# Retention and a gated-GELU MLP in fp32 on one core: three quarters of block 1's first product by seven products instead of eight, and a new order of the first steps

## The chip, the cores and the metric

The kernel runs on one core of a Trainium2 chip. The metric is the device time of one execution in microseconds. The engines are called TensorE (PE, with its weight loads PEld), VectorE (DVE), ScalarE (ACT), GpSimd (POOL) and SyncE (SP), which here only issues transfers.

## The reference

Four sequences of 768 positions go through eight heads of a recurrent retention of width 64. Its output, 3072 tokens of 512 numbers, goes through two matrices with a gate h * sigmoid(1.702 h) between them. All is float32.

```python
state = gamma * state + outer(k_t, v_t)          # per batch and head
y_t   = (1/8) * q_t @ state
x     = y, rearranged to (4*768, 8*64) = (3072, 512)
h     = x @ w_in                                 # (3072, 2048)
g     = h * (1 / (1 + exp(-1.702 * h)))
out   = g @ w_out                                # (3072, 512)
```

The weights come in as 64-bit floats and are narrowed to 32 bits on the chip.

## The kernel before

Tokens are worked on in six blocks of 512 (`CB` = 4 chunks of 128). A chunk is one of 12 pieces of 64 positions of two sequences; its attention is called a step. Block m+1's attention stands between the matmuls of block m's second product. Blocks 0 and 1 are different from the rest: while their attention and first products run, the weights are still being loaded and narrowed.

Matrices are split in two by two quarters. A product of two such matrices needs eight products of quarters, or seven if sums of quarters are formed first (the Winograd form of Strassen's scheme). The code keeps seven slots for each matrix: quarters 0 to 3, and sums 4, 5, 6; slot 2 is overwritten by a fourth sum, once nobody wants the quarter.

* `up0` makes a chunk of block 0's first product by plain products, `up1(f)` a chunk of 128 of the 2048 features for block 1: four matmuls of 128x512 (L427) into a PSUM tile `ph`, of tag `x` for even f and `y` for odd. `gate1.f` is ScalarE's gate on it, which writes `G`.
* `up(d)`, for blocks 2 to 5, makes four features' chunks at once by the seven products: 28 matmuls of 128x256 (L472). Three copies by ScalarE (`p1`, `u`, `vv`) and three adds by VectorE combine them. The sums of the weights (`sums_w1`) and of X (`sums_x`) stand in place by then.
* `down(m)` is the second product of blocks 0 and 1 by seven products (L709), each over 8 pairs of rows of W2; `sums_w2`, `sums_w2_t3` and `sums_g` make its sums on VectorE. A part of `sums_g` and `sums_w1` goes to GpSimd.
* A weight comes by `fetch` (SP, 512 KB in two transfers) to one of three raw places (`RAWS`: W2[:, 4], W2[:, 5], G[:, 6:8]), is begun by ScalarE (`abs`, L207), and finished by VectorE in `half` (L211 to L213) and `rest` (L217, L218, L222). Weights 0 to 7 are W1, 8 to 15 are W2.
* `X1`, block 1's input, lies in W2[:, 6], and is filled by steps 4 to 7 (`output`, called x4 to x7).

PSUM tiles of tags `x` and `y` have two buffers each; the tiles `q_sq` and `k_sq` (two buffers), `kn`, `tmp`, `kT` (one), `o`, `qT`, `at` (two) belong to the attention and to the outputs.

The order of everything up to block 1's gates is a list of words written out by hand. TensorE's order is the program's. `pin` puts an instruction of another engine behind the one that was traced before it on its engine; instructions without it (among them `aged` and `decay` on GpSimd from step 6 on, and the loads of step 8 and later) are placed by the scheduler, and what is pinned behind them goes with them. [...]

```python
for n, unit in enumerate(down(m) if m < 2 else down49(m, *ring)):
    unit()
    if m == 0 and n < NP and n % 2:
        sums_w2(n - 1)
```

Of the kernel before, what the change touches and what calls it, by code (L numbers as in the profile page):

```python
# [9 lines left out]
F32 = mybir.dt.float32  # L10
U32 = mybir.dt.uint32
AF = mybir.ActivationFunctionType
ALU = mybir.AluOpType
P = 128
# [14 lines left out]
def kernel(  # L29
# [29 lines left out]
    pe, act, dve, pool, sp = nc.tensor, nc.scalar, nc.vector, nc.gpsimd, nc.sync  # L59
# [10 lines left out]
    TH = BT // 2  # L70
    NB = NCH // CB
    NFF = DFF // P
    NP = NFF // 2
# [5 lines left out]
    one = ctx.enter_context(tc.tile_pool(name="one", bufs=1))  # L79
    two = ctx.enter_context(tc.tile_pool(name="two", bufs=2))  # L80
# [3 lines left out]
    ps = ctx.enter_context(tc.tile_pool(name="ps", bufs=2, space=bass.MemoryType.PSUM))  # L84
# [13 lines left out]
    G = const.tile([P, NP, 4, TH], F32, name="G")  # L98
    G0 = one.tile([P, 2, TH], F32, name="g0", tag="kd")
    X1 = W2[:, 6].rearrange("p (s c) t -> p s c t", s=4)  # L100
    rowd = const.tile([P, HP, D], F32, name="rowd")
# [3 lines left out]
    whole = const.tile([P, HP], F32, name="whole")  # L105
# [6 lines left out]
    def w1(p):  # L112

        return (W1A, p) if p < NP // 2 else (W1B[p // 2 - 2], p % 2)
# [3 lines left out]
    def pin(i):  # L118
        return tc.keep_in_program_order(i) if ordered[0] else i
# [58 lines left out]
    def fetch(i):  # L178
        x = raw(i).rearrange("p (n two) -> p n two", two=2)
        pin(sp.dma_start(x.rearrange("p (c f) two -> p c f two", c=2) if i < NFF else x, SRC[i]))  # L180
# [96 lines left out]
    def by_half(t, j):  # L277

        return t.rearrange("p s (w t) -> p w s t" if j < NEW else "p (w s) t -> p w s t", w=2)

    def attend(j, f=None):

        pa = ps_a.tile([P, 2, 2, HP, D], F32, name="pa", tag="pa")
        if j is not None:
            PA[j] = pa
            kt, qt = by_half(KT.pop(j), j), by_half(QT[j], j)
            for s in range(HP):
                for u, w in TWO:
                    pe.matmul(pa[HALF[w], u, 0, s, :], kt[HALF[u], w, s, :], qt[HALF[u], w, s, :], start=True, stop=True)  # L289
        if f is not None:  # L290
            c = f % NC
            old, vn, a, qt = state[c % 2], QKV.pop(("v", f)), AT.pop(f), by_half(QT.pop(f), f)
            if c < NC - 1:
                kd = KD.pop(f)
                for s in range(HP):
                    for w, u in TWO:
                        pe.matmul(pa[HALF[u], w, 1, s, :], kd[HALF[w], HP * u + s, :], vn[HALF[w], HP * u + s, :],
                                  start=True, stop=True)


            py = ps_a.tile([P, 2, 2, 4, D], F32, name="py", tag="py")
            if c:
                for s2 in range(2):
                    for w in range(2):
                        for u, o in TWO:
                            pe.matmul(py[HALF[o], u, 1, 2 * w + s2, :], old[HALF[u], w, 2 * s2 + o, :],  # L306
                                      qt[HALF[u], w, 2 * s2 + o, :], start=True, stop=True)
            for s2 in range(2):
                for u in range(2):
                    for w, o in TWO:  # L310
                        s = 2 * s2 + o
                        pe.matmul(py[HALF[o], w, 0, 2 * u + s2 if f < NEW else 2 * s2 + u, :],  # L312
                                  vn[HALF[w], HP * u + s, :], a[HALF[w], u, s, :], start=True, stop=True)
            PU[f], PY[f] = pa[:, :, 1], py
# [75 lines left out]
    def hidden(g, h):  # L390

        for g, i in g if isinstance(g, list) else [(g, slice(0, 2))]:
            pin(act.activation(g, h[:, i], AF.Gelu_apprx_sigmoid))  # L393
# [34 lines left out]
        return G[:, p, ab:4:2, :], h  # L428


    def sums_w1(p):
        t, q1 = w1(p)
        w = [t[:, q1:q1 + 2, s] for s in range(7)]
        pool.tensor_add(w[4], w[2], w[3])
        pool.tensor_sub(w[6], w[0], w[2])
        pool.tensor_sub(w[5], w[4], w[0])
        pool.tensor_sub(w[2], w[1], w[5])
# [310 lines left out]
    works, products = {}, {}  # L748
# [63 lines left out]
    for j in range(2 * CB):  # L812
        for name in "qkv":
            works[f"{name}{j}"] = lambda j=j, name=name: load(j, name)
        works |= {f"{name}{j}": lambda j=j, do=do: do(j) for name, do in (
            ("turn", turn), ("turned", turned), ("decay", decay), ("masked", masked), ("state", by_state),
            ("x", output), ("aged", aged), ("updated", updated))}
        for f in (None, *range(2 * CB)):
            works[f"step{j}" + ("" if f is None else f"-{f}")] = lambda j=j, f=f: attend(j, f)
        works[f"step-{j}"] = lambda j=j: attend(None, j)  # L820
    for i in range(2 * NFF):
        works[f"w{i // 2}{'ab'[i % 2]}"] = lambda i=i: fetch(i)
    for name, i in [("0a", 0), ("0b", 1)] + [(str(p), 2 * p) for p in range(1, NFF)]:
        n = Narrow(i)
# [19 lines left out]
    begin()  # L844
    for name in """
        k0 table q0 warm turn0 w0b rows warm k1 abs0b q1 turned0 step0 v0 w0a half0b mask k2 turn1 causal rest0b
        masked0 decay0 v1 decay1 abs0a half0a step-0 updated0 turned1 q2 step1 rowd whole w2b turn2 w2a x0 k3
        aged1 masked1 turned2 v2 rest0a abs2 q3 step-1 updated1 state1 decay2 aged2 step2 q4 x1 half2 decay3 w3b
        w3a up0.0.0 masked2 turn3 k4 step-2 v3 q5 rest2 k5 gate0.0.0 turned3 updated2 state2 step3 up0.0.2
        masked3 abs3 half3 x2 rest3 turn4 w1b step-3 aged3 gate0.0.2 turned4 state3 w1a w5b updated3 v5 decay4  # L850
        abs1 x3 turn5 half1 up0.0.3 turned5 up0.1.2 step4 aged4 w5a rest1 v4 gate0.0.3 decay5 w6a masked4
        gate0.1.2 abs5 w6b step5-4 half5 rest5 up0.0.1 updated4 abs6 state4 gate0.0.1 w4b
        up0.1.1 half6 aged5 w4a up0.0.5 rest6 masked5 up0.1.5 gate0.1.1 x4 gate0.0.5 abs4 step-5 w8b w8a
        half4 gate0.1.5 state5 updated5 anew q6 up0.1.6 x5 rest4 gate0.1.6 abs8 v6 up0.0.6 w7b w7a half8
        turn6 gate0.0.6 up0.1.0 abs7 half7 gate0.1.0 w9b w9a up0.1.4 q7 gate0.1.4 decay6 step6 masked6 rest7 up0.0.4 v7
        gate0.0.4 turn7 up0.1.3 gate0.1.3 aged6 step7-6 masked7 updated6 decay7 abs9 state6 x6 up0.0.7 rest8 gate0.0.7
        w11a w11b step-7 state7 x7 half9 w10b w10a up0.1.7 rest9 gate0.1.7 abs11 half11 up1.8 gate1.8
        w12a w12b rest11 up1.5 gate1.5 up1.4 gate1.4 abs10 half10 up1.0 gate1.0 rest10 up1.3 gate1.3 abs12
        aged7 updated7 up1.2 gate1.2 w14b w14a half12 up1.6 gate1.6 rest12 up1.9 gate1.9 abs14 half14 w13a w13b
        up1.11 gate1.11 rest14 up1.10 gate1.10 abs13 half13 w15a w15b up1.7 gate1.7 rest13 abs15 half15 up1.12  # L860
        gate1.12 late_loads up1.13 gate1.13 rest15 up1.15 gate1.15 up1.14 gate1.14 up1.1 gate1.1
    """.split():
        works[name]()
    ordered[0] = False
    INNER = [(0, 19), (0, 22), (0, 26), (1, 2), (1, 12), (1, 15), (1, 18)]
    for m in range(NB):
# [30 lines left out]
# [4 lines that stand above are left out]
            if m == 0 and NP <= n < 3 * NP // 2:  # L901
                sums_w2_t3(2 * (n - NP))
            if m == 1 and n % 8 == 3:
                sums_w1(n // 4)
            if (m, n) in INNER:
                inner_w2(INNER.index((m, n)))
            if between and (n in (2, 5, 11, 16, 21) if m == 1 else n % 3 == (1 if m else 2)):
                between.pop(0)()
            if 0 < m < NB - 1 and n == (23 if m == 1 else 11):
                sums_x()  # L910
# [46 lines left out]
```

## Time and profile before

| what | value |
|---|---|
| median of three runs | 667.8 us (666.75 to 668.11) |
| the profiled execution | 667.55 us, span 665.8 us |
| granted clock of TensorE | 0.995 of full |
| block 1's first product (L427) | 104.17 to 159.11 us |
| the second product of block 0 (L709) begins | 159.11 us |
| first product of block 2 (L472) begins | 265.94 us |
| L211, L212, L217 on 128x1024 | 0.69 us each |
| L213, L218, L222 on 128x1024 | 1.23 us each |

A line of the timeline has the start and the length in us, the engine, the line of the kernel, the operation, what it writes and reads with the size, and how many it merges; in brackets stand the idle time before it and what ended it. A line of the chain of waits has start, length and what was waited for.

### The profile page before, as it was taken

Reading aid. Unit: us, or ns where it says so; the run is one execution under the profiler, and the core shown is the slowest. Engines: PE = TensorE matmul, PEld = TensorE weight load, DVE = VectorE, ACT = ScalarE, POOL = GpSimd, SP = SyncE. Lnnn points to the kernel's source line nnn. Section 1 sums busy time; section 2 is a strip of 40 time slices with the busy share of each in tenths; the row PEclk is TensorE's granted clock in tenths of the full one; section 3 lists DMA queues with packets and bytes.
Section 4 is the critical chain, followed back from the end, with each engine's and each line's share of the span. In section 5 each row is a group of like instructions: output and inputs, shape, how many; then the busy total and the mean of one; then the engine's idle time right before and its main releaser. Section 6 shows DMA issues by size and latency. Waiting matters only on the chain.

```text
span 665.8 us, 14995 instructions
## 1 busy us (share of the span) xinstructions
PE 645.9 (97%) x6294; PEld 559.1 (84%) x6294; DVE 435.1 (65%) x618; ACT 148.2 (22%) x285; POOL 188.7 (28%) x216
## 2 busy tenths in 40 slices
PE   6789999999999999999999999999999999999997
PEld 3678875446888888888999888999888999988997
DVE  3699878788545775456985354995264995254965
ACT  4674322231000000233100233110233110233110
POOL 6400310000268326100445600354700255500000
PEclk9799999999999999999999999999999999999999
DMA  9996637542203546263385742286652143502142
GB/s 174 205 256 178 186 68 231 166 87 38 43 11 133 172 109 189 56 226 123 89 215 132 230 116 94 75 204 150 189 163 95 62 148 113 222 32 94 49 158 96
DMA packets 146083, 89.48 MB, mean 134 GB/s; under 512 B 131456, under 2 KB 132736, under 8 KB 144992
## 3 DMA queue, kind: packets, MB, share of 16 engines
q1 hardware_dynamic: 135856, 45.19, 30.0%
q0 software_dynamic: 7824, 42.10, 17.8%
q10 hardware_dynamic: 2336, 1.25, 0.6%
q8 instruction: 49, 0.80, 0.5%
q14 instruction: 18, 0.15, 0.1%
HBM read 72.89 MB, written 15.47 MB: 133 GB/s over the span
## 4 chain that ended last, share of the span: by engine, by line
PE 80%; DMA 8%; DVE 4%; SPq 3%; POOL 3%; issue 1%; ACT 0%; DVEq 0%; POOLq 0%; ACTq 0%
PE pq L576 21%; PE px L472 16%; PE pd L709 13%; PE py L472 12%; PE ph L427 8%; PE ph L414 4%; DMA W<-in_moe_w_in_dram 2%; PE pa L289 2%; DMA W<-in_moe_w_out_dram 1%; SPq L157 1%; DMA G<-in_moe_w_in_dram 1%; DMA kn_in<-in_k_dram 1%; PE py L312 1%; PE py L306 1%; DMA k_sq<-in_k_dram 1%
## 5 line engine op out<-in xcount | busy, mean ns | idle before, releaser
L576 PE MATMUL pq<-W,G 128*128 128x128 f32 x672 | 80.5, 276 | 0.7 <-issue 0.7
L545 POOL DMA_DIRECT2D ring<-W2D x28 | 15.4, 552 | 228.9 <-PE px L472 118.2
L576 PEld LDWEIGHTS pq<-W,G 128*128 128x128 f32 x672 | 77.6, 192 | 1.5 <-issue 0.9
L472 PE MATMUL px<-X,W1A 128*128 128x256 f32 x256 | 60.0, 380 | 0.8 <-POOL X L442 0.7
L472 PE MATMUL px<-X,W1B 128*128 128x256 f32 x256 | 59.8, 379 | 0.0
L576 PE MATMUL pq<-ring,own 128*128 128x128 f32 x448 | 59.8, 276 | 0.0
L472 PEld LDWEIGHTS px<-X,W1A 128*128 128x128 f32 x256 | 48.3, 190 | 7.9 <-POOL X L442 1.6
L576 PEld LDWEIGHTS pq<-ring,own 128*128 128x128 f32 x448 | 54.5, 192 | 0.4
L472 PEld LDWEIGHTS px<-X,W1B 128*128 128x128 f32 x256 | 48.6, 190 | 6.7
L709 PE MATMUL pd<-W,G 128*128 128x256 f32 x224 | 49.6, 381 | 0.0
L709 PEld LDWEIGHTS pd<-W,G 128*128 128x128 f32 x224 | 42.2, 190 | 5.8
L472 PE MATMUL py<-X,W1A 128*128 128x256 f32 x192 | 45.4, 379 | 0.0
L472 PE MATMUL py<-X,W1B 128*128 128x256 f32 x192 | 45.4, 379 | 0.0
L393 ACT ACTIVATE G<-G 128x512 f32<-128x512 f32 x48 | 30.2, 630 | 52.0 <-DVE G L482 33.4
L472 PEld LDWEIGHTS py<-X,W1A 128*128 128x128 f32 x192 | 36.5, 190 | 5.0
L472 PEld LDWEIGHTS py<-X,W1B 128*128 128x128 f32 x192 | 36.5, 190 | 4.9
L490 DVE TENSOR_TENSOR t<-py,u 128x512 f32<-128x512 f32 x16 | 11.1, 692 | 33.2 <-PE py L472 33.2
L479 ACT ACTIVATE p<-px 128x512 f32<-128x512 f32 x16 | 9.6, 597 | 94.5 <-PE px L472 94.5
L414 PE MATMUL ph<-X,W1A 128*128 128x256 f32 x128 | 29.0, 382 | 1.4 <-DVE X L347 0.8
L576 PE MATMUL pq<-ring,G 128*128 128x128 f32 x224 | 29.6, 275 | 0.0
L576 PE MATMUL pq<-W,own 128*128 128x128 f32 x224 | 29.6, 275 | 0.0
L504 DVE TENSOR_TENSOR G<-G 128x512 f32<-128x512 f32 (+2 forms) x24 | 12.3, 513 | 25.7 <-ACT G L393 25.7
(207 smaller groups left out, 1168.3 us busy)
## 6 DMA issues: line engine op xcount, KB each, us to landing
ring<-W2D POOLq DMA_DIRECT2D x28, 768.0 KB, 4.7
W1B<-W1D POOLq DMA_DIRECT2D x6, 1792.0 KB, 9.3
W<-in_moe_w_in_dram SPq DMA_DIRECT2D x12, 512.0 KB, 5.3
W<-in_moe_w_out_dram SPq DMA_DIRECT2D x10, 512.0 KB, 5.0
out_dram<-o POOLq DMA_DIRECT2D x20, 256.0 KB, 3.2
q_sq<-in_q_dram SPq DMA_DIRECT2D x144, 32.0 KB, 2.2
k_sq<-in_k_dram SPq DMA_DIRECT2D x144, 32.0 KB, 2.2
v_in<-in_v_dram SPq DMA_DIRECT2D x72, 64.0 KB, 2.7
```

The lines of the kernel that those rows point to most:

```text
L157: tc.keep_in_program_order(sp.dma_start(t[r0:r0 + C4, :, n], src[b + r0 // D, :, t0:t0 + C4, r0 % D:r0 % D + C4] .rearrange("h p d -> p h ...
L289: pe.matmul(pa[HALF[w], u, 0, s, :], kt[HALF[u], w, s, :], qt[HALF[u], w, s, :], start=True, stop=True)
L393: pin(act.activation(g, h[:, i], AF.Gelu_apprx_sigmoid))
L414: pe.matmul(h[:, ab], w, X[:, 2 * th + c // 2, c % 2, :], start=(ab == 0 and c == 0), stop=(c == 3), skip_group_check=True)
L427: pe.matmul(h, w, X1[:, c // 2:4:2, c % 2, :], start=(c == 0), stop=(c == 3))
L472: pe.matmul(acc[:, u, :], t[:, q1 + u, sa, c, :], X[:, sb, c, :], start=(start and u == 0 and c == 0), stop=(stop and c == 1), skip_group_ ...
L479: act.activation(p1, x, AF.Copy)
L490: dve.tensor_add(tt, z, u)
L504: dve.tensor_sub(q[0][1], q[0][0], q[0][1])
L545: pool.dma_start(c, W2D[i])
L576: pe.matmul(p0[:, j, :], a[:, d], w[:, d], start=(new and j == 0 and d == 0), stop=(d == NP // 2 - 1), skip_group_check=True)
L709: pe.matmul(p0[:, n, :], g1(m, p, sa)[:, n * P:(n + 1) * P], W2[:, sb, p, :], start=(new and p == 0 and n == 0), stop=(last and p == NP - ...
```

## The change

Twelve of block 1's sixteen chunks (f = 0 to 11) are made by seven products, in groups of four, in the order d = 2, 0, 1. Chunks 12 to 15 stay as they were. Since W1's rows and X1 are needed as they are, the sums go to tiles that are idle at that time: those of X1 to `q_sq`, `k_sq`, `kn` and `tmp`, those of the weights to `qT`, `at`, `o` and `kT`. All are made by GpSimd: 4 for X1, and 4 for each d. The weights 11, 10, 12, 14, 13, 15 are narrowed between the products, as before, in this order. `late_loads` (step 8's and 9's first loads) moves behind the last of the three groups; decay 3 moves behind the first gate; step-0, turn 1 and step 1 move ahead, and q2 ahead of v1.

```diff
+    def seven_x():
+        for n, (tag, bufs) in ((4, ("q_sq", 2)), (5, ("k_sq", 2)), (6, ("kn", 1)), (2, ("tmp", 1))):
+            SUM_X[n] = two.tile([P, 2, TH], F32, name=f"x{n}", tag=tag, bufs=bufs)
+        for to, a, b in ((SUM_X[4], X1[:, 2], X1[:, 0]), (SUM_X[5], X1[:, 3], SUM_X[4]),
+                         (SUM_X[6], X1[:, 3], X1[:, 2]), (SUM_X[2], X1[:, 1], SUM_X[5])):
+            pin(pool.tensor_sub(to, a, b))
+    def seven_w(d):
+        t, q1 = w1(2 * d)
+        w = [t[:, q1:q1 + 2, s].rearrange("p u c f -> p u (c f)") for s in range(4)]
+        SUM_W[d] = {4: one.tile([P, 2, 2 * P], F32, name="w4", tag="qT", bufs=2),
+                    5: one.tile([P, 2, 2 * P], F32, name="w5", tag="at", bufs=2),
+                    6: two.tile([P, 2, 2 * P], F32, name="w6", tag="o"),
+                    2: one.tile([P, 2, 2 * P], F32, name="w2", tag="kT")}
+        m = SUM_W[d]
+        pin(pool.tensor_add(m[4], w[2], w[3]))
+        pin(pool.tensor_sub(m[5], m[4], w[0]))
+        pin(pool.tensor_sub(m[6], w[0], w[2]))
+        pin(pool.tensor_sub(m[2], w[1], m[5]))
+    def seven(d, k):
+        t, q1 = w1(2 * d)
+        a = [G[:, 2 * d:2 * d + 2, s, :] for s in range(4)]
+        def product(acc, sa, sb, start, stop):
+            for u in range(2):
+                for c in range(2):
+                    w = SUM_W[d][sa][:, u, c * P:(c + 1) * P] if sa in (4, 5, 6, 2) else t[:, q1 + u, sa, c, :]
+                    x = SUM_X[sb][:, c, :] if sb in SUM_X else X1[:, sb, c, :]
+                    pe.matmul(acc[:, u, :], w, x, start=(start and u == 0 and c == 0), stop=(stop and c == 1),
+                              skip_group_check=True)
+        def kept(name, tag, src):
+            SEVEN[name] = one.tile([P, 2, TH], F32, name=name, tag=tag)
+            pin(act.activation(SEVEN[name], src, AF.Copy))
+        if k in (0, 1, 3, 5):
+            SEVEN["x" if k == 0 else f"y{k}"] = ps.tile([P, 2, TH], F32, name="ph", tag="x" if k == 0 else "y")
+        acc = SEVEN[f"y{k}" if k in (1, 3, 5) else "x"]
+        product(acc, (0, 1, 5, 4, 6, 2, 3)[k], (0, 1, 5, 4, 6, 3, 2)[k], k in (0, 1, 3, 5), k in (1, 3, 5, 6))
+        if k == 0:
+            kept("p1", "s1", acc)
+        elif k == 1:
+            pin(dve.tensor_add(a[0], acc, SEVEN["p1"]))
+            hidden(a[0], a[0])
+        elif k == 2:
+            kept("u", "s2", acc)
+        elif k == 3:
+            SEVEN["t"] = one.tile([P, 2, TH], F32, name="t", tag="s1")
+            pin(dve.tensor_add(SEVEN["t"], acc, SEVEN["u"]))
+        elif k == 4:
+            kept("vv", "s3", acc)
+        elif k == 5:
+            pin(dve.tensor_add(a[3], SEVEN["y3"], SEVEN["vv"]))
+            hidden(a[3], a[3])
+            pin(dve.tensor_add(a[2], acc, SEVEN["t"]))
+            hidden(a[2], a[2])
+        else:
+            hidden(a[1], acc)
...
-        masked0 decay0 v1 decay1 abs0a half0a step-0 updated0 turned1 q2 step1 rowd whole w2b turn2 w2a x0 k3
-        aged1 masked1 turned2 v2 rest0a abs2 q3 step-1 updated1 state1 decay2 aged2 step2 q4 x1 half2 decay3 w3b
-        w3a up0.0.0 masked2 turn3 k4 step-2 v3 q5 rest2 k5 gate0.0.0 turned3 updated2 state2 step3 up0.0.2
+        masked0 decay0 q2 v1 step-0 updated0 turned1 decay1 step1 rowd masked1 abs0a half0a whole w2b turn2 w2a x0 k3
+        aged1 turned2 v2 rest0a abs2 q3 step-1 updated1 state1 decay2 aged2 step2 q4 x1 half2 w3b
+        w3a up0.0.0 masked2 turn3 k4 step-2 v3 q5 rest2 k5 turned3 gate0.0.0 decay3 updated2 state2 step3 up0.0.2
...
-        w11a w11b step-7 state7 x7 half9 w10b w10a up0.1.7 rest9 gate0.1.7 abs11 half11 up1.8 gate1.8
-        w12a w12b rest11 up1.5 gate1.5 up1.4 gate1.4 abs10 half10 up1.0 gate1.0 rest10 up1.3 gate1.3 abs12
-        aged7 updated7 up1.2 gate1.2 w14b w14a half12 up1.6 gate1.6 rest12 up1.9 gate1.9 abs14 half14 w13a w13b
-        up1.11 gate1.11 rest14 up1.10 gate1.10 abs13 half13 w15a w15b up1.7 gate1.7 rest13 abs15 half15 up1.12
-        gate1.12 late_loads up1.13 gate1.13 rest15 up1.15 gate1.15 up1.14 gate1.14 up1.1 gate1.1
+        w11a w11b step-7 state7 x7 half9 w10b w10a seven_w2 up0.1.7 rest9 gate0.1.7 abs11
+        seven_x seven2.0 seven2.1 half11 seven2.2 seven2.3 w12a w12b rest11 seven2.4 seven2.5 aged7 seven_w0 abs10 seven2.6
+        seven0.0 seven0.1 half10 seven0.2 seven0.3 rest10 w14b w14a seven0.4 seven0.5 seven_w1 abs12 seven0.6
+        updated7 seven1.0 seven1.1 half12 seven1.2 seven1.3 rest12 w13a w13b seven1.4 abs14 seven1.5 half14
+        seven1.6 up1.12 rest14 gate1.12 abs13 half13 w15a w15b late_loads up1.13 gate1.13 rest13 abs15 half15
+        up1.15 gate1.15 rest15 up1.14 gate1.14
```

In `seven`, `seven2.0` is the first of the seven products of d = 2, and so on. Lines of the changed kernel below `up1` stand 67 later, so that L458 becomes L525.

More of the change, by code (lines that the diff above doesn't have):

```diff
@@ L428, in up1 @@
         return G[:, p, ab:4:2, :], h
+    SUM_X, SUM_W = {}, {}
+    def seven_x():
[16 more added lines that the diff above has]
+        pin(pool.tensor_sub(m[2], w[1], m[5]))
@@ new lines @@
+    SEVEN = {}
+    def seven(d, k):
[34 more added lines that the diff above has]
+            hidden(a[1], acc)
@@ L820 @@
         works[f"step-{j}"] = lambda j=j: attend(None, j)
+    works["seven_x"] = seven_x
+    for d in range(NP // 2):
+        works[f"seven_w{d}"] = lambda d=d: seven_w(d)
+        for n in range(7):
+            works[f"seven{d}.{n}"] = lambda d=d, n=n: seven(d, n)
     for i in range(2 * NFF):
```

## The prediction

> **What bounds the kernel now.** I read the page's busy times first, then TensorE's timeline from 100 us on, then the chain of waits.
>
> ```profile
> PE 645.9 (97%) x6294; PEld 559.1 (84%) x6294; DVE 435.1 (65%) x618; ACT 148.2 (22%) x285; POOL 188.7 (28%) x216
> ```
>
> TensorE is the bound as a whole. In the stage that changes it has no gap, so here a matmul less is time less, as long as nothing else is late:
>
> ```profile
> 104.17 3.60 PE L427 MATMUL ph<-W,W1B 128*128 128x512 f32 x8
> ...
> 155.67 3.60 PE L427 MATMUL ph<-W,W1A 128*128 128x512 f32 x8
> 159.11 3.62 PE L709 MATMUL pd<-W,W1A 128*128 128x256 f32 x16
> ...
> 186.62 1.99 PE L709 MATMUL pd<-W,W1B 128*128 128x256 f32 x8 [0.28 <-DVE W1B L458]
> ...
> 265.94 1.89 PE L472 MATMUL px<-X,W1A 128*128 128x256 f32 x8
> 267.67 1.89 PE L472 MATMUL py<-X,W1A 128*128 128x256 f32 x8
> ```
>
> Each f32 matmul leaves two records. A chunk of L427 (4 matmuls, 8 records) takes 3.433 us from start to start: (159.11-104.17)/16. One of the seven products of a later block (8 records of half the width) takes 267.67-265.94 = 1.73 us; 28 of them, 265.94 to 314.29, give 1.727. In 186.62, VectorE (the sums of G) is already the last to arrive.
>
> In the first 44 us the chain of waits runs through loads of W1:
>
> ```profile
> 8.39 10.16 DMA W<-in_moe_w_in_dram
> ...
> 18.56 8.73 DMA G<-in_moe_w_in_dram
> ...
> 30.56 5.77 DMA W<-in_moe_w_in_dram
> ```
>
> Last, what GpSimd and VectorE do to each other, from their timelines:
>
> ```profile
> 76.58 0.78 DVE L212 TENSOR_SCALAR W<-W 128x1024 uint32<-128x1024 uint32 x1
> 77.39 1.94 DVE L213 SCALAR_TENSOR_TENSOR G<-G,W 128x1024 uint32<-128x1024 uint32 x1
> ...
> 95.21 0.68 DVE L368 TENSOR_TENSOR state<-state,pa 128x512 f32<-128x512 f32 x1
> ```
>
> ```profile
> 76.89 1.35 POOL L274 TENSOR_TENSOR G<-kn_in,cold 128x512 f32<-128x512 f32 x1
> 78.21 2.01 POOL L359 TENSOR_TENSOR state<-state,whole_h 128x512 f32<-128x512 f32 x1
> 95.33 1.04 POOL L274 TENSOR_TENSOR G<-kn_in,cold 128x512 f32<-128x512 f32 x1 [15.11 <-DMA kn_in<-in_k_dram]
> ...
> 190.10 2.48 POOL L434 TENSOR_TENSOR W1B<-W1B 128x512 f32<-128x512 f32 x2
> ```
>
> The bracket has the idle time before an instruction and what ended it. At 77 us L213 needs 1.94 us where it takes 1.23 elsewhere: it starts behind GpSimd's L274, and GpSimd's L359 behind it needs 2.01 instead of 1.04. At 95 us the same L274 beside L368 (which reads PSUM) costs neither anything. A sum such as the new ones takes GpSimd 1.24 us alone (L434).
>
> [...]
>
> **The change part by part.**
>
> *Products.* Removed: 12 chunks, 12 x 3.433 = 41.2 us. Added: 21 products, 21 x 1.727 = 36.3 us. Saved on TensorE: **4.9 us**, if it never waits.
>
> *Sums on GpSimd.* 16 instructions (4 of X1, 4 for each of 3 pairs of chunk rows), 16 x 1.25 = 20 us. In the order in which the changed kernel's instructions stand on POOL, they come after decay 7 (ends 96.4 us): four of seven_w2, aged 7, three of seven_w0, and only then the four of seven_x. TensorE's third product (seven2.2) needs x5, the tenth of these. Alone: 96.4 + 9 x 1.25 + 1.04 = 108.7, and TensorE wants it at 104.17 + 2 x 1.73 = 107.6: 1.1 us late[...]. But VectorE stands in L217 to L222 of rest8 and in half9 and rest9, nine instructions[...]. Both queues are full, so they alternate: a VectorE instruction waits about 0.93 us (1.25 less the 0.3 by which neighbours overlap: L213 above, and pairs of L522 with L436 at 212 us repeat every 1.70 us), a GpSimd one 0.4 to 0.95 us. Ahead of x5, by who stands in front: 0.4, 0.9 and 0.9 for the last three of seven_w2, nothing for aged 7 (VectorE then reads PSUM), 0.4, 0.4 and 0.9 for seven_w0, 0.4 and 0.9 for x4 and x5: 5.2 us, so x5 at 114.0. **TensorE waits 6.4 us.**
>
> *VectorE behind it.* Its nine instructions lose 8 us: rest9 ends at 115.1 instead of 108.0. Then a0 add (0.7), half11 (2.7, waits 1.2), t add (0.7), rest11 (3.2, waits 2.0 behind seven_w0's last and seven_w1), so that the add of a3 ends at 126.2. seven0.1 needs the PSUM tile which that add frees; TensorE comes to it at 114.0 + 6 x 1.73 = 124.4 and **waits 1.8**. The add of a2 ends at 126.9; behind it ScalarE has two gates, abs10 (1.1), gate a1 and the copy p1 of the next pair, 3 us: 129.8. seven0.2 overwrites that PSUM tile, comes to it at 128.0 and **waits 1.85**. From there GpSimd has two sums and aged 8 left and TensorE runs free. Sum: 10.1 waited, 4.9 saved: **5.1 us later** at the end of the twelve chunks.
>
> *The tail on VectorE.* In the old order VectorE had room before the second product (idle 6.6 us until 170.32, 2.4 and 1.0 us after it). Now rest12 to rest15 come late. From the end of seven1.5: two adds 1.8, weight 14 5.95, wait for its gate and abs13 1.8, weights 13 and 15 11.9, then the sums of W2 (16), four transposes, mask and one output, 13.0: 34.4 us. Then the twelve sums of G, 10.9 us as at 175.67 to 186.57, and a transpose of k that now stands between them, 0.65: 46.0. TensorE reaches the same point after 1.7 + 13.7 + 27.2 (159.11 to 186.34) = 42.7. It waits 3.4 us instead of 0.28: **3.1 us** more, whatever happened before. Bound: 0 if VectorE catches up by another order, 4 if the transposes' loads come late as well.
>
> *ScalarE and VectorE's own work:* 9 copies of 0.6 us on an engine 22% busy, hidden apart from the wait above; 12 adds of 0.69 (8.3 us) are in the sums above. The gates stay in number.
>
> *kn of step 8* leaves SP ahead of w11 (2.6 us of issuing at 97.21) for a place behind w13, as its tile now holds x6. w11 could come earlier, but it needs rest8 done (102.5): it lands near 108, abs11 ends at 109 and p1 at 109.7, before 114.0. Costs nothing; were rest8 not delayed, w11 would be issued at 100.6, and p1 done by 107.5, just in time too. *late_loads* and w15 move behind rest12 (about 149): their 32 issues of 4 to 5 us per eight end near 170, and the last transpose is due at 184. Nothing.
>
> *First steps.* step-0, turn 1 and step 1 run some 5 us earlier; q2 goes ahead of v1 on SP, both still ahead of w2, so w2 is issued at the same place. ScalarE's abs2 still waits for w2 (27.38), VectorE's masked2 still stands behind half2, and up0.0.2 waits for rest2 at 36.3 as before. decay3 moves behind gate0.0.0, into ScalarE's wait for w3. I take **0**; bounds -3 (up0.0.0 at 25.4 instead of 28.3, should that reach the end) and +0.5.
>
> **Sum**, against the profiled execution (667.55, of which the span is 665.8; the median of the runs is 667.8, 0.25 more): -4.9 + 10.1 + 3.1 = +8.2, so 675.8 us.
>
> **Rivals.**
> 1. *The sums are covered* (faster). If GpSimd's sums do not meet VectorE, only the tail is left: -4.9 + 3.1 = -1.9 with no wait for x5, 665.7. For it: POOL is idle from 97.4 to 123.4. Against: VectorE is busy nearly without a break from 95 to 108. It decides if x5 comes before about 109.5. Chance 0.08.
> 2. *The first steps pay* up to 3 us and the sums little: 663 to 665. Against: three loads in the chain. 0.05.
> 3. [...] fewer collisions than full queues give, waits 3 to 6 us shorter: 669.5 to 673. 0.20.
> 4. *Ends alike* within 1.3 us: 0.05.
> The forecast, with all its waits, 0.62, own range 673 to 679.5.
>
> **The numbers.** Faster 0.08 + 0.05 = 0.13; same 0.05; slower 0.62 + 0.20 = 0.82 (0.2%, 1.3 us, is about what a measurement can tell). The range 668.5 to 679.5 leaves out rivals 1 and 2 and a little above.
>
> **What would show it.** Right: seven products of 1.73 us; TensorE idle for over 4 us before the third of them, released by POOL x; L217 to L222 at 96 to 116 us near 1.6 to 2.2 us instead of 0.69 to 1.23; seven0.1 and seven0.2 waiting for VectorE and ScalarE; over 2 us of waiting for W1B L525 in the second product; abs2 at 27.4 still. Wrong: x5 done by 109, or the first L414 after rest3 clearly before 44 us.

## The result, and the profile after

The changed kernel takes **671.8 us** (median of 4 runs, 671.23 to 672.95) against 667.3 for the kernel before beside it (666.65 to 668.11): a ratio of **1.0069**, 95% interval 1.0050 to 1.0088. It is 4.5 us slower. The profiled execution took 671.79 us, with a span of 670.1.

By the page TensorE is busy for 1.7 us less, VectorE for 15.0 and GpSimd for 26.8 us more. Slow and held-up time counts as busy in these sums: TensorE is busy for 2.00 of the 2.00 us from 115 to 117 at a granted clock of 0.50, VectorE's L222 at 112.55 counts 2.17 us instead of 1.23, and GpSimd's L439 at 113.60 counts 2.25 instead of 1.26.

```profile
PE 644.2 (96%) x6366; PEld 574.3 (86%) x6366; DVE 450.1 (67%) x630; ACT 153.0 (23%) x294; POOL 215.5 (32%) x232
```

The lines of the changed kernel that matter: L467 is a product of `seven`, L472 ScalarE's copies (p1, u, vv), L481, L487, L491 and L493 are VectorE's adds out of PSUM (a0, t, a3, a2). On GpSimd L439 makes the four sums of X1, the second of which is x5, and L450 to L453 the four sums of a pair's weights. In the second product (L776) L514 to L516 are the sums of W2 and L519 is t3 (`sums_w2_t3`), L523 to L525 are the sums of G on VectorE, and L529 is the part of them on GpSimd. "The stage" is block 1's first product, and "the tail" block 0's second product behind it.

TensorE's timeline, in the stage and then in the tail:

```profile
103.68 3.62 PE L467 MATMUL ph<-W,W1B 128*128 128x256 f32 x16
113.69 7.30 PE L467 MATMUL ph<-x,w 128*128 128x256 f32 x24 [6.39 <-POOL x L439]
120.83 1.89 PE L467 MATMUL ph<-W,w 128*128 128x256 f32 x8
122.55 1.89 PE L467 MATMUL ph<-x,W1B 128*128 128x256 f32 x8
...
127.73 5.34 PE L467 MATMUL ph<-x,w 128*128 128x256 f32 x24
...
148.45 13.90 PE L427 MATMUL ph<-W,W1B 128*128 128x512 f32 x32
```

```profile
186.58 1.99 PE L776 MATMUL pd<-W,W1A 128*128 128x256 f32 x8 [0.87 <-DVE W1A L525]
189.46 1.99 PE L776 MATMUL pd<-W,W1B 128*128 128x256 f32 x8 [0.88 <-DVE W1B L525]
191.73 1.99 PE L776 MATMUL pd<-W,W1B 128*128 128x256 f32 x8 [0.28 <-DVE W1B L525]
```

Read the starts, not the lengths. A product of 8 records takes 1.72 us (120.83 to 122.55). TensorE stops for 6.39 us before the third product, and then the next 24 records last from 113.69 to 120.83, 7.14 us, where the same 24 take 5.18 further down (127.73 to 132.91). Stretches of TensorE's time (the stretch, its length, busy time with the number of records, granted clock, DMA share, GB/s) say why:

```profile
109.00:111.00 2.00, 0.00 (x0) 0.91 0.70 109
111.00:113.00 2.00, 0.00 (x0) 0.50 0.00 0
113.00:115.00 2.00, 1.31 (x3) 0.50 0.00 0
115.00:117.00 2.00, 2.00 (x6) 0.50 0.64 127
117.00:119.00 2.00, 2.00 (x10) 0.88 0.96 393
```

The granted clock went to 0.50 while TensorE stood still, and it stayed there until past 117 us, for nearly the first 4 us of work.

So the stage, from its first product to the first of block 0's second product (162.19), takes 58.51 us against 54.94 before: 4.94 saved by the products, 6.56 lost at the stop, and 1.96 to the slow clock. From there to block 2's first product it is 108.86 against 106.83, 2.03 more. The stage starts 0.49 earlier, and the rest, from block 2's beginning on, is 0.81 shorter. Sum: +3.57 + 2.03 - 0.49 - 0.81 = 4.3, the difference of the two spans.

GpSimd and VectorE in the stage:

```profile
98.74 2.25 POOL L452 TENSOR_TENSOR w<-W1B 128x512 f32<-128x512 f32 x1
...
111.51 2.12 POOL L439 TENSOR_TENSOR x<-W,x 128x512 f32<-128x512 f32 x1
113.60 2.25 POOL L439 TENSOR_TENSOR x<-W 128x512 f32<-128x512 f32 x1
...
122.80 1.52 POOL L453 TENSOR_TENSOR w<-W1A,w 128x512 f32<-128x512 f32 x1 [5.28 <-PE ph L467]
```

```profile
110.35 2.17 DVE L218 SCALAR_TENSOR_TENSOR W<-W 128x1024 f32<-128x1024 uint32 x1
112.55 2.17 DVE L222 TENSOR_TENSOR W<-W 128x1024 f32<-128x1024 f32 x1
114.64 0.68 DVE L481 TENSOR_TENSOR G<-ph,p 128x512 f32<-128x512 f32 x1
...
121.96 1.23 DVE L222 TENSOR_TENSOR W<-G 128x1024 f32<-128x1024 f32 x1
123.10 0.69 DVE L491 TENSOR_TENSOR G<-ph,vv 128x512 f32<-128x512 f32 x1
```

A sum of 1.26 us takes up to 2.25, and L218 and L222 take 2.17 instead of 1.23. VectorE loses nothing at L481, which reads PSUM while a sum of GpSimd's runs (0.68 us), nor at L222 at 121.96, where GpSimd stands idle for most of the time (1.23 us).

VectorE in the tail, in the kernel before and then in the changed one (the last instruction on a weight, t3, the first sum of G):

```profile
150.91 1.23 DVE L222 TENSOR_TENSOR W<-W 128x1024 f32<-128x1024 f32 x1
...
160.59 2.49 DVE L452 TENSOR_TENSOR W<-W 128x512 f32<-128x512 f32 x4
...
175.67 0.69 DVE L456 TENSOR_TENSOR X<-W1A,X 128x512 f32<-128x512 f32 x1 [0.98 <-PE pd L709]
```

```profile
166.69 1.23 DVE L222 TENSOR_TENSOR W<-W 128x1024 f32<-128x1024 f32 x1
...
176.96 1.89 DVE L519 TENSOR_TENSOR W<-W 128x512 f32<-128x512 f32 x3
...
180.60 0.65 DVE L523 TENSOR_TENSOR X<-W1A,X 128x512 f32<-128x512 f32 x1
```

Before, the last weight was done 7.0 us ahead of the second product's first matmul (159.11); now it is done 5.7 us behind it (162.19). Before, t3 ran in time that VectorE had to spare; now it stands ahead of sums of G that TensorE waits for, and the first of these starts 18.4 us into the product instead of 16.6.

### The profile page after: what moved, and what is told of

It is laid out like the page before. It is cut to its first block, busy times and chain, and to the rows that moved or that the text cites. A ratio compares the mean times of both kernels' runs of the same rounds, so it can differ in the third digit from the quotient of the medians.

```text
span 670.1 us, 15199 instructions
## 1 busy us (share of the span) xinstructions
PE 644.2 (96%) x6366; PEld 574.3 (86%) x6366; DVE 450.1 (67%) x630; ACT 153.0 (23%) x294; POOL 215.5 (32%) x232
## 4 chain that ended last, share of the span: by engine, by line
PE 81%; DMA 7%; DVE 4%; POOL 4%; SPq 1%; issue 1%; ACT 1%; ACTq 0%; POOLq 0%; DVEq 0%
PE pq L643 24%; PE px L539 16%; PE pd L776 13%; PE py L539 12%; PE ph L467 5%; PE ph L414 4%; PE ph L427 2%; DMA W<-in_moe_w_in_dram 2%; DMA kn_in<-in_k_dram 2%; PE pa L289 2%; DMA G<-in_moe_w_in_dram 1%; DMA W<-in_moe_w_out_dram 1%; PE py L312 1%; DMA k_sq<-in_k_dram 1%; PE py L306 1%; PE pa L297 1%
## 5 line engine op out<-in xcount | busy, mean ns | idle before, releaser
L393 ACT ACTIVATE G<-G 128x512 f32<-128x512 f32 x57 | 35.7, 630 | 67.6 <-DVE G L549 33.4
L776 PE MATMUL pd<-W,G 128*128 128x256 f32 x224 | 49.6, 381 | 0.0
L776 PEld LDWEIGHTS pd<-W,G 128*128 128x128 f32 x224 | 42.2, 190 | 5.9
L557 DVE TENSOR_TENSOR t<-py,u 128x512 f32<-128x512 f32 x16 | 11.1, 692 | 33.3 <-PE py L539 33.3
L414 PE MATMUL ph<-X,W1A 128*128 128x256 f32 x128 | 30.0, 392 | 0.9 <-DVE W1A L222 0.8
```

What stands on the lines that cost most here:

```text
L414: pe.matmul(h[:, ab], w, X[:, 2 * th + c // 2, c % 2, :], start=(ab == 0 and c == 0), stop=(c == 3), skip_group_check=True)
L557: dve.tensor_add(tt, z, u)
L776: pe.matmul(p0[:, n, :], g1(m, p, sa)[:, n * P:(n + 1) * P], W2[:, sb, p, :], start=(new and p == 0 and n == 0), stop=(last and p == NP - ...
```

## The experiments

Every kernel ran beside the kernel before on the same chip; ratios are to that.

### The two parts of the change

`e1_order_only`: the kernel before with the new order of the first steps.

```diff
-        masked0 decay0 v1 decay1 abs0a half0a step-0 updated0 turned1 q2 step1 rowd whole w2b turn2 w2a x0 k3
...
+        masked0 decay0 q2 v1 step-0 updated0 turned1 decay1 step1 rowd masked1 abs0a half0a whole w2b turn2 w2a x0 k3
...
```

> The kernel before with the new order of the first steps alone. Theory (the loads of W1 bound the first 44 us): 666.8 us, 0.5 under before, since the first chunk of block 1's product began 0.49 us earlier in the changed kernel. Rival (the early steps are worth what they move, about 3 us): 664.3 us.

Measured: 667.40 us, 1.0009 (0.9990 to 1.0027). The first steps bring nothing that can be measured.

`e2_seven_only`: the changed kernel with the old order of the first steps (the same words the other way round).

> The changed kernel with the old order of the first steps: the seven products alone. Theory: 0.5 us above the changed kernel, 672.3 us, with the same wait of 6.4 us for a sum of X1. Rival (the new order costs something that the products hide): 671 us or less.

Measured: 670.79 us, 1.0057 (1.0040 to 1.0073), an interval that overlaps that of the whole change. TensorE's stop is 6.55 us here, the tail's waits 0.86, 0.89 and 0.28. The loss belongs to the seven products. (TensorE's stop is its wait for x5, the tail's waits are those for L525.)

### What holds TensorE in the stage

`e4_no_narrow`: rest8, half9 and rest9 left out, the VectorE work that stands beside GpSimd's first sums. Weights 8 and 9 stay unfinished, so this kernel has less to do than the others and its time is not that of a whole one; what it shows is GpSimd's sums and TensorE's wait.

```diff
-        gate0.0.4 turn7 up0.1.3 gate0.1.3 aged6 step7-6 masked7 updated6 decay7 abs9 state6 x6 up0.0.7 rest8 gate0.0.7
-        w11a w11b step-7 state7 x7 half9 w10b w10a seven_w2 up0.1.7 rest9 gate0.1.7 abs11
+        gate0.0.4 turn7 up0.1.3 gate0.1.3 aged6 step7-6 masked7 updated6 decay7 abs9 state6 x6 up0.0.7 gate0.0.7
+        w11a w11b step-7 state7 x7 w10b w10a seven_w2 up0.1.7 gate0.1.7 abs11
```

> The changed kernel without rest8, half9 and rest9: nine instructions of VectorE on weights 8 and 9, which are left unfinished, so the result is not the reference's. They stand beside GpSimd's sums. Theory [...]: GpSimd's sums up to x5 take 1.25 to 1.35 us each instead of 1.6 to 2.25, x5 is done near 108.4, TensorE waits about 1.2 us there, and the whole takes about 664.7 us. Rival (the sums are slow by themselves, or the matmuls' reads slow them): they stay at 1.6 to 2.25 us and TensorE waits over 4 us.

Measured: 663.98 us, 0.9938 (0.9912 to 0.9964). GpSimd's and then TensorE's timeline of it:

```profile
100.24 1.26 POOL L453 TENSOR_TENSOR w<-W1B,w 128x512 f32<-128x512 f32 x1
...
107.62 1.26 POOL L439 TENSOR_TENSOR x<-W,x 128x512 f32<-128x512 f32 x1
```

```profile
108.94 5.45 PE L467 MATMUL ph<-x,w 128*128 128x256 f32 x24 [1.04 <-POOL x L439]
```

Without VectorE's narrowing every sum up to x5 takes 1.26 to 1.28 us and TensorE waits 1.04 us, and the 24 records behind the wait take 5.28 us (108.94 to 114.22), not 7.14. What remains of the stop is the number of sums ahead of x5; the other 5.35 us are collisions. TensorE's matmuls run beside the sums here too (L414 for 3.72 us from 100.72 on, beside sums of 1.26 us), so it is not they that make the sums slow.

`e3_x_first`: the four sums of X1 ahead of those of pair 0 on GpSimd, so that x5 is three sums earlier. (Aged 7 is not pinned and runs early; the three sums of pair 0 that were pinned behind it went with it. With the two words exchanged they stay behind X1's.)

```diff
-        seven_x seven2.0 seven2.1 half11 seven2.2 seven2.3 w12a w12b rest11 seven2.4 seven2.5 aged7 seven_w0 abs10 seven2.6
+        seven_x seven2.0 seven2.1 half11 seven2.2 seven2.3 w12a w12b rest11 seven2.4 seven2.5 seven_w0 aged7 abs10 seven2.6
```

> The changed kernel with the four sums of X1 ahead of the three sums of seven_w0 on GpSimd (two words of the order exchanged). Rival A (the place of x5 in GpSimd's queue is the whole loss): the wait of 6.4 us and the slow matmuls behind it go, 663.5 us. Theory B (VectorE, held up by GpSimd, comes next): x5 is done near 108 us, but the adds of a0 and a3 still end near 115 and 123.8, so TensorE waits about 2 us for the PSUM tile of seven2.5 and 1.8 us for that of seven0.1, and seven0.1 starts near 124 instead of 126: about 669.8 us.

Measured: 673.35 us, 1.0088 (1.0067 to 1.0109). Both expectations (663.5 and 669.8) were too low. x5 was done at 107.03 and TensorE no longer waits for it, but:

```profile
108.17 3.69 PE L467 MATMUL ph<-x,w 128*128 128x256 f32 x16 [1.53 <-ACT p L472]
116.09 3.21 PE L467 MATMUL ph<-x,w 128*128 128x256 f32 x8 [4.23 <-ACT u L472]
...
126.60 1.97 PE L467 MATMUL ph<-W,W1A 128*128 128x256 f32 x8 [1.68 <-DVE G L491]
129.85 5.42 PE L467 MATMUL ph<-x,w 128*128 128x256 f32 x24 [1.28 <-ACT p L472]
```

The copy p stands behind abs11 on ScalarE, which waits for weight 11, whose load is issued at 101.57, when rest8 is done (101.54). The copy u stands behind the gate of a0, which waits for VectorE's add (114.12), which stands behind half9 and rest9, whose six instructions all meet a sum of GpSimd's. These two waits are 5.76 us together, nearly as long as the stop for x5 had been, and the last two (1.68 and 1.28) come on top. So by the timelines the collisions on VectorE make several things late at once, and when x5 is no longer the last of them, TensorE meets the next.

`f1_warm`: seven matmuls of ident by ident, which nobody needs, fill the stop.

```diff
-        seven_x seven2.0 seven2.1 half11 seven2.2 seven2.3 w12a w12b rest11 seven2.4 seven2.5 aged7 seven_w0 abs10 seven2.6
+        seven_x seven2.0 seven2.1 half11 warm_py seven2.2 seven2.3 w12a w12b rest11 seven2.4 seven2.5 aged7 seven_w0 abs10 seven2.6
...
+        for i in range(7):
+            pe.matmul(t, ident, ident[:, None, :].to_broadcast([P, 4, P]), start=True, stop=True)
```

> The kernel after, with seven matmuls of ident by ident (128x512 f32, 0.86 us each, 6.0 us in all) on TensorE between seven2.1 and seven2.2, into the idle PSUM tile py; nothing reads their result. Theory (the 6.4 us without work left TensorE at half its clock for the next 4 us, and that cost 1.95 us of the 24 records behind the wait): those 24 records take 5.2 us instead of 7.14 and the clock column stays at 1.00. TensorE then comes to seven0.1 at about 124.1 instead of 126.0, VectorE's add of a3 ends there at 123.8 to 124.8 because GpSimd's L453 now starts some 1.9 us earlier, into rest11: a new wait of about 0.7 us. Net 1.2 us less than after: 670.5 us. Rival (the slow stretch was hidden by what VectorE and ScalarE were late with, so that its end changes nothing): the waits at seven0.1 and seven0.2 come back in full, 1.9 us, and the time stays at 671.8.

Measured: 673.50 us, 1.0096 (1.0077 to 1.0116), an interval that overlaps that of the changed kernel: nothing was gained, as the rival said. TensorE's timeline, then VectorE's:

```profile
108.31 6.17 PE L893 MATMUL warm<-ident 128*128 128x512 f32 x14
114.78 5.45 PE L467 MATMUL ph<-x,w 128*128 128x256 f32 x24 [0.30 <-POOL x L439]
120.07 1.89 PE L467 MATMUL ph<-W,w 128*128 128x256 f32 x8
...
125.85 1.97 PE L467 MATMUL ph<-W,W1A 128*128 128x256 f32 x8 [0.44 <-DVE G L491]
129.02 5.45 PE L467 MATMUL ph<-x,w 128*128 128x256 f32 x24 [1.21 <-ACT p L472]
```

```profile
122.92 2.17 DVE L222 TENSOR_TENSOR W<-G 128x1024 f32<-128x1024 f32 x1
125.02 0.68 DVE L491 TENSOR_TENSOR G<-ph,vv 128x512 f32<-128x512 f32 x1
```

The granted clock stays at 1.00 from 107 to 133 us, and the 24 records take 5.29 us, 1.85 less than in the changed kernel. But GpSimd's L453, which waits for TensorE to let go of its tile, now starts at 122.04 (1.93 us earlier, counted from the stage's first product) and meets L222, which takes 2.17 instead of 1.23. seven0.1 starts 0.60 us late and seven0.2 another 1.44: 2.04 lost for 1.85 gained. From the first product to the second product of block 0 it is 58.72 us, against 58.51. So the slow clock was real, but taking it away gained nothing here: two waits for VectorE and ScalarE come in its place.

### The tail

`f2_t3_late`: the four instructions of `sums_w2_t3` behind the sums of G.

```diff
-        dve.tensor_sub(W2[:, 6, p:p + 2, :], W2[:, 5, p:p + 2, :], W2[:, 0, p:p + 2, :])
+        tc.keep_in_program_order(dve.tensor_sub(W2[:, 6, p:p + 2, :], W2[:, 5, p:p + 2, :], W2[:, 0, p:p + 2, :]))
...
-            if m == 0 and NP <= n < 3 * NP // 2:
-                sums_w2_t3(2 * (n - NP))
+            if m == 0 and 3 * NP // 2 <= n < 2 * NP:
+                sums_w2_t3(2 * (n - 3 * NP // 2))
```

> The kernel after, with the four instructions of sums_w2_t3 (L519, 4 x 0.6 us on VectorE) behind the twelve sums of G instead of ahead of them and among them. Theory (the tail is a matter of VectorE's order between 176 and 191 us: 2.4 us of sums that nobody needs before the sixth product stand ahead of sums that TensorE waits for): the three waits for L525, 2.03 us in all, fall to 0.3 or less, and the time is 1.7 us less than after: 670.0 us. Rival (VectorE's work as a whole is late, rest15 ends at 168 while TensorE begins the second product at 162, and what is moved is waited for later): the waits turn up at the products behind, 671.8 us.

Measured: 670.91 us, 1.0060 (1.0042 to 1.0079): too small a step to tell from none by the times. In the trace the tail, up to block 2's first product, is 108.02 us instead of 108.86: TensorE waits once, 1.82 us for W1B L525, instead of three times, 2.03 in all. VectorE is in time now (its first L523 waits 0.98 us for TensorE, as in the kernel before), but meets GpSimd's L529 on the way (L524 takes 1.64 us three times of four and L525 1.63 once, instead of 0.69):

```profile
178.93 0.69 DVE L523 TENSOR_TENSOR X<-W1A,X 128x512 f32<-128x512 f32 x1 [0.98 <-PE pd L776]
...
187.71 1.64 DVE L524 TENSOR_TENSOR W1B<-W1B 128x512 f32<-128x512 f32 x1
189.38 1.63 DVE L525 TENSOR_TENSOR W1B<-g,W1B 128x512 f32<-128x512 f32 x1
```

`g1_tail`: as `f2_t3_late`, with L529 on VectorE behind them.

```diff
-        tc.keep_in_program_order(pool.tensor_sub(a[1], a[1], a[0]))
+        tc.keep_in_program_order((pool if m else dve).tensor_sub(a[1], a[1], a[0]))
```

> As f2_t3_late, and the four sums of L529 (a1, 128x512, none of them needed before the seventh product) on VectorE behind the sums of G and t3, instead of on GpSimd among them. In f2_t3_late GpSimd's L529 starts as soon as L525 is done and meets L524 and L525, which take 1.64 us there instead of 0.69, four times. Theory [...]: L524 and L525 take 0.69 us throughout, the wait of 1.82 us for W1B L525 is gone, and the time is 1.8 us less than f2_t3_late's 670.9: 669.1 us. Rival (VectorE as a whole is late, from rest15's end on): the wait stays near 1.8, 670.9 us.

Measured: 672.42 us, 1.0078 (1.0051 to 1.0104), above both expectations, though the interval overlaps that of `f2_t3_late`. L524 and L525 take 0.69 us and TensorE waits for none of them, as the theory said; but L529 on VectorE now meets GpSimd's sums of W1 (3.43 us for two of them at 199.90), and TensorE waits 0.79, 0.19 and 0.61 us for VectorE in the next product. How the one leads to the other over the 39 us between them was not followed; that it does is shown by `h2_tail`, which moves L529 off VectorE again and has none of these waits.

`h2_tail`: as `f2_t3_late`, with L529 back on GpSimd in the reverse order; the first then needs the last L525.

```diff
-                        for p in range(0, NP, 2):
+                        for p in range(0, NP, 2) if m else range(NP - 2, -1, -2):
```

> As f2_t3_late (the seven stage is that of the kernel after), with L529 on GpSimd in the reverse order as in h1_cover. Theory [...]: no wait for L525 (2.03 us in after, 1.82 in f2_t3_late) and no new wait in the next product (0.79, 0.19 and 0.61 in g1_tail), TensorE comes to the first product of block 2 106.8 us after it began the second product of block 0, against 108.9 in after: 669.0 to 669.8 us. Rival (VectorE's lateness): waits near 1.8 us stay or turn up at the next sums, 671 us.

Measured: 668.83 us, 1.0028 (1.0012 to 1.0043), 0.2 us under the theory's range. No wait in the tail, and none in the next product; 163.57 to 269.51 is 105.94 us, 2.92 less than after and 0.89 less than before. The stage keeps its stop (6.59 us). The last weight is done 5.73 us behind the second product's first matmul, exactly as in the changed kernel, and yet nothing waits. So VectorE's lateness costs time only together with the tail's old order, t3 ahead of sums that are waited for and L529 among them. That order is the same in the kernel before, where it costs only 0.28 us because VectorE is early.

### Other orders of the stage

`f3_best`: the same instructions as after in the stage, ordered so that X1's sums follow the first pair's, adds out of PSUM stand ahead of narrowing and the copy u ahead of the gate; the tail as in `f2_t3_late`.

```diff
             pin(dve.tensor_add(a[0], acc, SEVEN["p1"]))
-            hidden(a[0], a[0])
         elif k == 2:
             kept("u", "s2", acc)
+            hidden(a[0], a[0])
...
+        w11a w11b step-7 state7 x7 half9 w10b w10a seven_w2 seven_x up0.1.7 gate0.1.7
+        seven2.0 seven2.1 rest9 seven2.2 abs11 seven2.3 w12a w12b half11 seven2.4 seven_w0 aged7 seven2.5 rest11 w14b w14a
...
```

> The kernel after with its seven stage in another order, same instructions: on GpSimd the four sums of X1 directly behind seven_w2; on VectorE each add out of PSUM ahead of the narrowing steps that it stood behind (a0 before rest9, t before half11, a3 and a2 before rest11, and so on for the other pairs); on ScalarE the copy u ahead of the gate of a0, abs11 behind them, abs10, abs12, abs14 in its idle stretches; t3 as in f2_t3_late. Theory (6.4 us of wait, 1.95 us of slow clock and 1.75 us of tail all come from orders, and not from the amount of work): x5 by 107.1, TensorE waits under 1.5 us in the stage and under 0.5 us in the tail, 663 us (662 to 665), which is below the kernel before (667.4). Rival ([...] the waits only move to its adds or to the tail): 667 us or more.

Measured: 669.39 us, 1.0031 (1.0015 to 1.0048): better than after, if only just (the two intervals do not touch), and still slower than before. The theory's 663 us is missed, the rival's 667 or more holds. x5 is in time, and TensorE runs through the first pair; then

```profile
121.27 2.48 PE L467 MATMUL ph<-W,W1A 128*128 128x256 f32 x8 [2.82 <-DVE G L491]
124.54 7.82 PE L467 MATMUL ph<-x,w 128*128 128x256 f32 x24 [0.80 <-POOL w L453]
```

```profile
118.35 2.17 DVE L213 SCALAR_TENSOR_TENSOR G<-G,W 128x1024 uint32<-128x1024 uint32 x1
120.44 0.68 DVE L491 TENSOR_TENSOR G<-ph,vv 128x512 f32<-128x512 f32 x1
```

With its sums packed closely, GpSimd runs without a gap from 95 to 124.6 us, and most of what VectorE does between its adds is stretched. The slow clock returned behind the 2.82 us (0.50 from 123 to 129 us): 24 records take 7.66.

`f4_x_vector`: as that, the four sums of X1 on VectorE, directly behind the output of step 7.

```diff
-            pin(pool.tensor_sub(to, a, b))
+            pin(dve.tensor_sub(to, a, b))
...
-        w11a w11b step-7 state7 x7 half9 w10b w10a seven_w2 seven_x up0.1.7 gate0.1.7
+        w11a w11b step-7 state7 x7 seven_x half9 w10b w10a seven_w2 up0.1.7 gate0.1.7
```

> As f3_best, but the four sums of X1 on VectorE (0.69 us each) directly behind the output of step 7, instead of on GpSimd. Theory (a collision costs VectorE about 0.95 us, more than the 0.69 us of doing the sum itself): VectorE is no later than in f3_best by the time of the tail, x5 is there by 105, and the time is within 1 us of f3_best: 663 us. Rival (the 2.8 us stand in front of half9 and the add of a0 on VectorE, and TensorE waits for that add): 1.5 to 3 us more than f3_best, 665 to 666 us.

Measured: 671.11 us, 1.0058 (1.0032 to 1.0084). The median lies 1.7 us above that of `f3_best`, but the intervals overlap, and the profiled execution (668.37 us) is one of the shortest: its stage takes 57.34 us, that of `f3_best` 57.25. So nothing was gained, and a loss is not shown. The four sums took 1.55, 1.42, 1.75 and 1.75 us instead of 0.69: they, too, ran beside GpSimd's instructions (1.27 to 1.72 us each there). TensorE waited 1.45 us for the add of a0 and 3.46 for that of a3.

`g2_cover`: two pairs by seven products, and pair 2's four plain chunks ahead of them as a cover for the sums; adds, narrowing and the copy u in the order of `f3_best`, and the tail of `g1_tail`. The weights are narrowed in another order (9 and 11 first, then 10, 14, 12, 13, 15).

```diff
+        w11a w11b step-7 state7 x7 half9 w10b w10a seven_w0 seven_x up0.1.7 gate0.1.7
+        up1.8 gate1.8 abs11 half11 up1.9 gate1.9 rest11 w14b w14a up1.11 gate1.11 rest9 w12a w12b abs10 up1.10 gate1.10 seven_w1 aged7
+        seven0.0 seven0.1 half10 seven0.2 seven0.3 rest10 w13a w13b seven0.4 abs14 seven0.5 seven0.6 half14
...
```

> Seven products for two pairs of chunk rows (0 and 1) instead of three, and the four chunks of pair 2 by eight products in place as in the kernel before, ahead of the seven stage: 13.7 us of TensorE's work that need no sum, under which GpSimd does the sums of pair 0 and of X1. VectorE's adds out of PSUM stand ahead of narrowing as in f3_best, and the tail is as in g1_tail. Less work saved: 2 x 1.63 = 3.3 us instead of 4.9. Theory (the change lost its gain because the sums had nothing to run under at that place[...]): x5 is there 5 us before it is wanted, no wait over 0.5 us in the seven stage, no slow clock, no wait in the tail (0.28 in the kernel before); 667.0 less 3.3 and 0.3: 663.5 us. Rival (VectorE has too little room for narrowing[...], wherever the sums stand): it is late with weights 14 and 15 for the second product, or with an add, by 3 us or more: 667 us or more.

Measured: 666.58 us, 0.9997 (0.9978 to 1.0017). The stage went as expected: one wait of 0.27 us, 52.2 us long instead of 54.9. The gain was lost in the next product, where TensorE waited 0.84, 0.40, 0.61 and 0.25 us, much as in `g1_tail`.

`h1_cover`: that, with the tail of `h2_tail`.

> As g2_cover, with the four sums of L529 back on GpSimd in the reverse order: the first of them needs VectorE's last L525, so that none starts among the sums of G. In g2_cover TensorE waited for nothing in the tail, but VectorE met GpSimd again at L529 (3.43 us for two of them at 194 us), and TensorE waited 0.84, 0.40, 0.61 and 0.25 us in the next product. Theory [...]: no wait in the tail, L524 and L525 at 0.69 us, and those four waits, 2.1 us, are gone: 666.6 less 2.1, 664.5 us, faster than the kernel before (667.1) by 0.3 to 0.5%. Rival (another transfer or sum is due there anyway): 666 us or more.

Measured: **663.07 us, 0.9948 (0.9928 to 0.9968)**, faster than the kernel before and, by the two ratios, than the changed one. TensorE's timeline of the stage, whole but for pieces without a wait:

```profile
102.91 13.91 PE L427 MATMUL ph<-W,W1B 128*128 128x512 f32 x32
...
120.11 5.34 PE L467 MATMUL ph<-x,w 128*128 128x256 f32 x24
...
132.66 5.42 PE L467 MATMUL ph<-x,w 128*128 128x256 f32 x24 [0.27 <-ACT p L472]
...
155.10 3.62 PE L776 MATMUL pd<-W,W1A 128*128 128x256 f32 x16
```

The stage is 52.19 us (54.94 before), from there to block 2 it is 105.94 (106.83 before): 3.64 us less in these two stretches; the medians of the whole differ by 4.1. The collisions are still there (GpSimd's sums take 1.59 to 2.25 us at 96 to 115 us); they lie under 13.7 us of matmuls that need none of the sums. How much comes from two pairs rather than three, how much from the cover and how much from the order of the adds, was not taken apart; a third pair behind the cover was not tried. Nor was the tail's new order tried on the kernel before, where up to 0.89 us may be had without any of the stage's seven products.

The profiled execution took 665.74 us, 2.7 more than the median, and its span is only 2.0 us below that of the kernel before (663.8 against 665.8), though block 2 begins 4.9 us earlier. The other 2.9 us are lost again later:

```profile
469.54 3.58 PE L539 MATMUL px<-X,W1A 128*128 128x256 f32 x8 [3.35 <-POOL X L509]
```

At block 4's third product TensorE waits 3.35 us for a sum of X on GpSimd (0.69 at the same place before), and the 8 records behind the wait last 3.58 us instead of the usual 1.89; the page shows a granted clock of 0.8 in the slice from 464.7 to 481.3 us, and 0.9 or more in every other. GpSimd had waited 5.10 us for a load of kn ahead of that sum (4.63 before, but there TensorE came to block 4 6.3 us later). From block 4's first product to block 5's it is 105.37 us against 101.02, 4.35 more. As an estimate, 665.74 less 4.35 is 661.4, close to the shortest of the 14 executions (660.98); whether those are without that wait, no trace shows. So once the stage is shorter, this load can become the next thing that is late.

## Why the prediction was right, and where it was not

The direction was right and the range, 668.5 to 679.5, holds the time. The predicted 675.8 was 4.0 too high, and the forecast's own range (673 to 679.5) missed it. The measured time falls into rival 3's interval, but rival 3's mechanism, half the collisions, is not what happened.

* **Products, 4.9 saved: right**, 4.94.
* **Wait for x5, 6.4: right**, 6.39. So was its working: expected collisions of 5.2 us ahead of x5, measured 5.3 as the excess of GpSimd's sums over 1.27 us. That all nine narrowing instructions would collide was the author's estimate; the trace of before had shown it for L213 (1.94 us instead of 1.23), and that of the changed kernel shows it for all nine (16.62 us instead of 8.91). Also right were rest9's end at 115.1, measured 114.7, and the 1.1 us of lateness without collisions, 1.04 in `e4_no_narrow`. The nine narrowing instructions lost 7.7 us, expected 8. Rival 1 (covered sums) needs x5 before 109.5; it came at 113.6.
* **seven0.1 and seven0.2, 1.8 and 1.85: the step that failed.** In the changed kernel neither waited. The prediction priced TensorE's return at full speed; its clock was at half, which cost 1.96 us. TensorE's last work ahead of the stop ends at 107.30; the granted clock is 0.91 from 109 to 111 us, 0.50 from 111 to 117 and 0.88 from 117 to 119. The clock alone would not have put it right: `f1_warm` shows that with the clock kept up the two waits do come, 0.60 and 1.44 us, and together they cost as much as the slow clock did. The two waits together were priced at 3.65 and measured 2.04, chiefly since rest11 met GpSimd once (0.94 us) and not for 2.0 us. So the prediction had these waits about 1.6 us too long and left out the clock, which in the changed kernel gave VectorE the time to be ready. That the sum of the stage comes out within 1.5 us, 10.05 against 8.52, is in part luck.
* **The tail, 3.1 more: right in kind, 1.1 too much.** TensorE waits 2.03 us against 0.28, and the stretch up to block 2 is 2.03 longer. The waits are the same to 0.02 us in `e2_seven_only`, `e3_x_first`, `f1_warm` and even `e4_no_narrow`, whose stage is 7 us shorter, as "whatever happened before" said. VectorE's list of work was right too: from the end of seven1.5 (146.73) to the first sum of G (180.60) it took 33.9 us, priced at 34.4, and the sums of G took 11.1, priced at 11.55. Five transposes stand in the sum, and only four in the trace. What the prediction named only as a bound ("0 if VectorE catches up by another order") is what `h2_tail` does: rest12 to rest15 are just as late there, and TensorE waits for nothing. Lateness is the cause only as long as t3 and L529 stand where they stood.
* **First steps, 0: right** (`e1_order_only`). The -0.49 us in the trace is less than what separates executions: across the profiles shown here that have the new first steps, the stage begins between 102.9 and 104.9 us.
* **The rest, -0.8:** from block 2's beginning to the end the span is 0.81 us shorter than before, 0.67 of it a gap "issue" at 338.08 us that the profile after does not have. It was not predicted, and no run here explains it; apart from `h1_cover`, this stretch is 398.0 to 400.0 us in all profiles.

By the two spans the prediction is 3.9 us too high (8.2 against 4.3): 1.5 of it is the stage's waits (10.05 against 6.56 and 1.96), 1.1 the tail (3.1 against 2.03), and 1.3 the start and the end.

## What to carry to other kernels

Work taken off the engine that bounds the kernel is a gain only as far as its preparation does not make the engines that feed it late. So lay out the preparing work instruction by instruction against what the other engine does beside it, and ask what TensorE can do meanwhile that needs none of it. When one delay holds up several engines, removing the first wait shows the next one: price the second and the third before you move the first, and look whether the collision that was moved off one path lands on another. And a stop of TensorE can have a second price in its clock: here 1.96 us behind a stop of 6.39, which counted for nothing, because other engines were late by as much (2.04 us in `f1_warm`).

## What the runs showed of the hardware that was not expected

* VectorE and GpSimd slowed each other where both had work queued. Nine narrowing instructions on VectorE (rest8, half9 and rest9 in the changed kernel) took 16.62 us beside GpSimd's sums instead of 8.91, and a sum on GpSimd up to 2.25 us instead of 1.26. Moving sums from GpSimd to VectorE (`f4_x_vector`) did not escape it: the four took 1.42 to 1.75 us there instead of 0.69, beside what is left on GpSimd.
* The granted clock fell to 0.50 at waits of 6.39 us (the changed kernel, 111 to 117 us), 4.23 (`e3_x_first`, 118 to 120) and 3.46 (`f4_x_vector`, 123 to 125), and it fell at the wait of 3.35 us in `h1_cover` (8 records at 469.54 in 3.58 us instead of 1.89). It also fell in `f3_best` behind a wait of 2.82 us: 1.00 from 119 to 121 us, 0.89 from 121 to 123 and 0.50 from 123 to 129, though TensorE had been at work again since 121.27. Shorter waits show no such fall: 24 records took 5.28 us behind 1.04 us (`e4_no_narrow`), the clock stayed at 1.00 behind 1.45 us (`f4_x_vector`, 113 to 119) and behind 1.53 and 1.68 us (`e3_x_first`, 108 to 112 and 126 to 128), and behind 1.82 us (`f2_t3_late`) the 24 records from 192.91 on took 5.18.
* The price of the slow clock varied: behind a stop of 6.39 to 6.59 us the same 24 records took 6.72 us (`e2_seven_only`), 7.14 (the changed kernel) and 7.71 (`h2_tail`) instead of 5.18.
